# The first MoE product of the last two batches by one level of Strassen

## Chip, core and metric

The kernel runs on one core of a Trainium2 chip. The metric is the device time of one execution in microseconds (us); less is better. Engines are named as in the profile: PE multiplies matrices (PEld is its weight load), DVE and ACT are the vector and the scalar engine, POOL is GpSimd, SP issues most of the DMAs. PE, DVE, ACT and POOL each take their instructions in the order in which they were issued.

## What is computed

Attention with normed q and k, then a two-layer product on its output. 8 batches, 12 heads, 448 positions, 64 per head; 3584 tokens of 768, inner width 2048, all inputs f32.

```
q_n, k_n = rmsnorm(q, g_q), rmsnorm(k, g_k)
attn = softmax(q_n @ k_n.T / 8)
x = (attn @ v)  -> 3584 x 768        # heads side by side
h = x @ w_in                         # 768 -> 2048, "first MoE product"
g = max(0.01 * h, h)
out = g @ w_out                      # 2048 -> 768
```

## The kernel before

The attention works in 24 units: unit u is batch u // 3 and a group of four heads. Each unit has four steps d = 0 to 3. A step issues score matmuls (`qk`, L185, `score`, L179) and the exponential on ACT (`ex`, L192). Step 0 also closes the unit before: the product with v (`pv`, L320), the column sums (`zcol`, L263), and the maximum that shifts the next unit's exponent (`shift_max`, L208, on DVE with `dg` in L221, then `shift_mm`, L226, a small matmul on PE that waits for `dg`). The units 4 to 22 are "narrow": their 1/sum is brought to all rows by a DMA (`zcol_inv`, L289), and POOL multiplies it in (`xmul_pool`, L302: one tensor_tensor of 896 elements a unit, f32 in, f16 out). The result x of a batch lies in `xts[b]`, transposed, 6 blocks of 128 rows and 448 tokens, f16. The last unit does this from PSUM on DVE (`xmul`, L330).

Later units are prepared beside that: sums of squares on DVE (`prep_ssq`, L140), 1/rms on ACT (`prep_rinv`, L145), the norm on DVE (`prep_norm`, L150: two inputs in SBUF, f32, output f16), a transpose by DMA (`prep_trd`, L165), and a scaling on DVE (`prep_g`, L137).

The MoE of batch b is a queue of items, pushed by `push` (L500) when the batch's last unit is nearly through (`fed`, L532: step 3 of the first unit of the next batch), and put between the attention's steps by `fill` (L535): each step gets a share of the queue by the items' costs (1.13 for an item of the first product, 1.31 for one of the second), and after each item one of the step's waiting jobs is issued. After step 3 of unit 23 what is left runs by itself; batch 7's MoE is that tail. So the order on every engine is written out by hand and by these costs.

The first product (`moe1`, L344) has 16 items a batch. Each takes one block of 128 output rows: 6 matmuls of 448 columns into one PSUM bank, then a leaky ReLU on ACT into `gt` (L342).

The second product (`seven`, L423) already uses one level of Strassen on pairs of token tiles: seven items i0 to i6 of 8 matmuls of 384 columns, in four PSUM banks `ma` to `md`. `ma`, `mc` and `md` are used twice: a first product is read out by DVE (L444, or `add`, L435), and a second is then accumulated on top of it in PSUM. The weights' differences are in `tw` (`weight_sum`, L399, 1536 f16 elements each on DVE), those of `gt` in `sa` (`s1` to `s4`, L408 to L418, DVE). What follows an item on DVE or ACT is kept in `pend` (`later`, L420) and issued by `flush` (L373) at the start of the next item.

PSUM has eight banks: two "slots" of two banks each for the scores, and four "aux" banks (`aux`, L55), which the framework hands out in turn.

Of the kernel before, what the change touches and what calls it, by code (L numbers as in the profile page):

```python
# [8 lines left out]
FP32 = mybir.dt.float32  # L9
FP16 = mybir.dt.float16  # L10
AF = mybir.ActivationFunctionType
ALU = mybir.AluOpType
# [6 lines left out]
def kernel(  # L19
# [11 lines left out]
    nc = tc.nc  # L31

    B, H, S, D = q.shape
    QH = 4
    NS = 7
    P = 128
    NQ = H // QH
    NU = B * NQ
    DM, DF = moe_w_in.shape
    KT = DM // P  # L40
    FT = DF // P
# [4 lines left out]
    raws = ctx.enter_context(tc.tile_pool(name="raws", bufs=3))  # L46
    prep_p = ctx.enter_context(tc.tile_pool(name="prep", bufs=2))
# [4 lines left out]
    opool = ctx.enter_context(tc.tile_pool(name="opool", bufs=4))  # L52
    psum = ctx.enter_context(tc.tile_pool(name="psum", bufs=1, space=bass.MemoryType.PSUM))

    def aux(shape, dtype, name):  # L55
        return psum.tile(shape, dtype, tag="aux", bufs=4, name=name)

    ident16 = cst.tile([P, P], FP16)
    make_identity(nc, ident16)
# [17 lines left out]
    win16 = cst.tile([P, NQ, 2, DF], FP16)  # L77
    wout16 = cst.tile([P, FT, DM], FP16)
    gt = cst.tile([P, FT, 8 * 64], FP16)
    HF = FT // 2  # L80
# [29 lines left out]
    def load_v(u):  # L110
# [8 lines left out]
        n16=([P, 2, NS, 2, D], FP16, 1), qkT=([P, 2, NS, P], FP16, 3))  # L119
# [56 lines left out]
    def slot():  # L176
        return psum.tile([P, 2, 512], FP32, tag="sT", bufs=2, name="sT")
# [67 lines left out]
    xts = {}  # L245
# [38 lines left out]
    def zcol_sum(u):  # L284
        s = st[u]
        s["zs"] = zpool.tile([P, HS], FP32, tag="zs", name="zs")
        nc.vector.tensor_reduce(s["zs"], s["zc"][:, 0:S].rearrange("p (k x) -> p x k", k=2), axis=AXL.X, op=ALU.add)

    def zcol_inv(u):  # L289
        s = st[u]  # L290
        nc.scalar.activation(s["zs"], s["zs"], AF.Ln)
        nc.scalar.activation(s["zs"], s["zs"], AF.Exp, bias=0.0, scale=-1.0)
        s["rz"] = zpool.tile([P, 2, S], FP32, tag="rz", name="rz")
        for r in range(2):
            for y in range(2):
                src = s["zs"][64 * y + r:64 * y + 64:2, None, :]
                nc.sync.dma_start(s["rz"][:, r, HS * y:HS * y + HS], src.broadcast_to([32, 4, HS]))
# [32 lines left out]
    def xmul(u):  # L330
        s = st[u]
        b, g = divmod(u, NQ)
        if b not in xts:
            xts[b] = xpool.tile([P, NQ, 2, S], FP16, tag="xt", name="xt")
        for r in range(2):
            nc.vector.tensor_tensor(xts[b][:, g, r], s["pv"][r][:, 0:S], s["rz"][:, r], op=ALU.mult)  # L336

    def prelu(b, dst, src):
        if b % 2 == 0:
            src = src.rearrange("p (t x) -> p t x", t=NS)[:, ::-1]  # L340
            dst = dst.rearrange("p (t x) -> p t x", t=NS)
        nc.scalar.activation(dst, src, AF.Prelu, bias=0.0, scale=1.0, alpha=0.01)  # L342
# [15 lines left out]
    def col(t):  # L358
        return 64 * (5 - 2 * t) if t < 3 else P * (t - 3)
# [10 lines left out]
    pend = []  # L370
    L, R, LR = slice(0, HC), slice(HC, DM), slice(0, DM)

    def flush():  # L373
        while pend:
            pend.pop(0)()

    def out_tile():
        return opool.tile([P, DM], FP32, tag="ost", name="ost")

    def moe2(pair, t, half, part):  # L380
        flush()
        if half == 0 and part == 0:
            ost[0] = out_tile()
        if part == 0:
            ost[1] = aux([P, 512], FP32, "op2")
        op2 = ost[1]
        for ft in range(8 * part, 8 * part + 8):
            nc.tensor.matmul(op2[:, 0:HC], gt[:, ft, ds(col(t), P)], wout16[:, ft, ds(HC * half, HC)],  # L388
                             start=(ft == 0), stop=(ft == FT - 1))
        if part == 0:  # L390
            return
        nc.vector.tensor_copy(ost[0][:, ds(HC * half, HC)], op2[:, 0:HC])
        if half == 1:
            store(pair, t, ost[0], LR, False)

# [24 lines left out]
    def later(fn, *args):  # L420
        pend.append(lambda: fn(*args))

    def seven(pair, tt, nxt=None, last=False):  # L423
        g = {}

        def mm(bank, a, b, first):
            for f in range(HF):
                nc.tensor.matmul(bank[:, 0:HC], a[:, f], b[:, f], start=(first and f == 0), stop=(f == HF - 1), skip_group_check=not first)  # L428

        def bank(name):  # L430
            g[name] = aux([P, 512], FP32, name)
            return g[name]

        def add(dst, src, name):
            nc.vector.tensor_tensor(dst, g[name][:, 0:HC], src, op=ALU.add)  # L435

        def put(i, c):
            store(pair, tt[i], g["o"][i], c, last)

        def i0():  # L440
            flush()
            g["o"] = (out_tile(), out_tile())
            mm(bank("ma"), gblock(tt[0], 0), wblock(0, 0), True)
            later(lambda: nc.vector.tensor_copy(g["o"][1][:, L], g["ma"][:, 0:HC]))  # L444

        def i1():
            flush()
            mm(bank("mb"), sa[:, 1], tw[:, 1], True)
            later(lambda: add(g["o"][1][:, L], g["o"][1][:, L], "mb"))

        def i2():
            flush()
            mm(g["ma"], gblock(tt[0], 1), wblock(1, 0), False)
            later(lambda: nc.scalar.copy(g["o"][0][:, L], g["ma"][:, 0:HC]))  # L454
            if last:
                later(put, 0, L)

        def i3():
            flush()
            mm(bank("mc"), sa[:, 0], tw[:, 0], True)  # L460
            later(lambda: add(g["o"][1][:, R], g["o"][1][:, L], "mc"))
            if nxt:
                later(s1, nxt)

        def i4():
            flush()
            mm(bank("md"), sa[:, 2], tw[:, 2], True)
            later(lambda: add(g["o"][1][:, R], g["o"][1][:, R], "md"))
            if last:
                later(put, 1, R)  # L470

        def i5():
            flush()
            mm(g["mc"], sa[:, 3], wblock(1, 1), False)
            if nxt:
                later(s2, nxt)
            later(lambda: add(g["o"][0][:, R], g["o"][1][:, L], "mc"))
            later(put, 0, R if last else LR)
            if nxt:
                later(s3, nxt)  # L480
                later(s4, nxt)

        def i6():
            flush()
            mm(g["md"], gblock(tt[1], 1), tw[:, 3], False)
            later(lambda: add(g["o"][1][:, L], g["o"][1][:, L], "md"))
            later(put, 1, L if last else LR)

        return [i0, i1, i2, i3, i4, i5, i6]

    queue = []

# [7 lines left out]
    def push(b):  # L500
        pair, odd = divmod(b, 2)
        fast = b > 0
        order = [f // 2 + HF * (f % 2) for f in range(FT)] if odd else range(FT)
        items = [(1.13, lambda ft=ft: (flush(), moe1(b, ft))) for ft in order]
        half = [(slice(0, 4)), (slice(4, 8))]
        if odd:
            tt, tn = (3, 4), (5, 6)
            items += [(1.31, fn) for fn in seven(pair, tt, tn)]
            for n, x, fs in ((8, 0, (s1, s2)), (10, 0, (s3, s4)), (FT - 1, 1, (s1, s2)), (FT, 1, (s3, s4))):
                c, fn = items[n]  # L510
                items[n] = (c, also(fn, *[lambda f=f, x=x: later(f, tt, half[x]) for f in fs]))
            items += [(1.31, fn) for fn in seven(pair, tn, None, b == B - 1)]
        else:
            tiles = (2,) if fast else (0, 1, 2)
            std = [lambda t=t, h=h, p=p: moe2(pair, t, h, p) for t in tiles for h in range(2) for p in range(2)]
            if fast:
                tt = (0, 1)
                std[0] = also(std[0], lambda: later(s1, tt))
                std[1] = also(std[1], lambda: later(s2, tt))
                std[2] = also(std[2], lambda: later(s3, tt), lambda: later(s4, tt))  # L520
                std += seven(pair, tt)
            items += [(1.31, fn) for fn in std]
        queue.extend(items)
# [53 lines left out]
    with tc.manual_schedule():  # L577
# [172 lines left out]
        first = slot()  # L750
# [9 lines left out]
        for u in range(3, NU):  # L760
            for d in range(4):
# [18 lines left out]
                def job(fn, *args):  # L780
                    jobs.append(lambda: fn(*args))
# [37 lines left out]
                    job(weight_sum, u - 5, 1)  # L819
                if d == 2 and 5 <= u < 8:  # L820
                    job(xmul_sb, u - 1)
                if d == 3 and 6 <= u < NU - 3:
                    for ti in range(2):
                        job(prep_sq, u + 3, ALL, (ti,))
# [2 lines left out]
        pv(NU - 1)  # L827
        zinv(NU - 1)
        xmul(NU - 1)
        push(B - 1)  # L830
        while queue:
            queue.pop(0)[1]()
# [29 lines left out]
```

## Time and profile before

| what | value |
|---|---|
| median of 3 runs | 424.19 us (424.12 to 425.42) |
| profiled execution | 424.41 us, of which the span of the trace is 422.6 |
| DMA | 62.37 MB, mean 148 GB/s |
| first product, L348 on PE | 756 matmuls recorded, 151.2 us |
| its leaky ReLU, L342 on ACT | 126 of 448 elements, 66.4 us, 547 ns each |
| POOL's multiplication, L307 | 16 of 896 elements, 33.7 us, 2104 ns each |
| `weight_sum`, L403 on DVE | 8 of 1536 elements, 0.946 us at the least |
| batch 6, first product | 340.1 to 362.8 us of the span, between the steps of units 22 and 23 |
| batch 7, first product | 381.8 to 400.0 us, alone on PE |

Busy times are those of one execution. An engine's row names the source line, the operation, output and inputs, and the shape. A row of the timeline starts with the start in us from the span's start and the duration in us; "[0.31 <-ACT rinv L148]" is idle time of the engine before the row and what ended it. A PE row's end holds the depth of the array, some 0.16 us that the next matmul overlaps. Idle time of an engine that nothing waits for costs nothing.

### The profile page before, as it was taken

How to read it: one execution, taken by the hardware profiler on the slowest of the kernel's cores; microseconds unless marked ns; L12 is line 12 of the kernel's file. 1: busy time of each engine (PE TensorE's matmuls, PEld its weight loads, DVE VectorE, ACT ScalarE, POOL GpSimd, SP SyncE). 2: the span in 40 equal slices, each digit the busy share in tenths (PEclk: the TensorE clock that was granted, in tenths of full speed). 3: DMA queues.
4: the chain of work that ended last, by engine and by line, in shares of the span. 5: the costliest groups of instructions: out<-in, count | busy, mean ns of one | idle time of the engine just before them, and what ended most of it. 6: DMA issues, size and time to landing. Idle time of an engine off the chain costs nothing.

```text
span 422.6 us, 8871 instructions
## 1 busy us (share of the span) xinstructions
PE 407.0 (96%) x3623; PEld 207.3 (49%) x3623; DVE 256.2 (61%) x417; ACT 302.9 (72%) x470; POOL 83.3 (20%) x75
## 2 busy tenths in 40 slices
PE   7887999989999999999999999999999999999995
PEld 6554454444445544454445544454445544555563
DVE  5788675888568736576459736577449721531262
ACT  5999877768987689877887689867986566733400
POOL 1957432200020121210220220210120101200000
PEclk9699999999999999999999999999999999999999
DMA  7999996889664995677664795677542460213023
GB/s 269 228 250 259 237 253 90 209 150 198 165 152 74 213 247 94 160 185 166 155 148 74 211 216 118 172 164 175 156 79 45 123 158 2 45 37 76 0 57 94
DMA packets 71947, 62.37 MB, mean 148 GB/s; under 512 B 36324, under 2 KB 67044, under 8 KB 71908
## 3 DMA queue, kind: packets, MB, share of 16 engines
q1 hardware_dynamic: 61312, 49.62, 46.1%
q0 software_dynamic: 10272, 11.80, 17.8%
q8 instruction: 28, 0.46, 0.5%
q10 hardware_dynamic: 324, 0.39, 0.3%
q14 instruction: 11, 0.09, 0.1%
HBM read 45.61 MB, written 11.01 MB: 134 GB/s over the span
## 4 chain that ended last, share of the span: by engine, by line
PE 83%; DVE 8%; ACT 6%; issue 1%; DMA 1%; SPq 0%; DVEq 0%
PE hps L348 34%; PE sT L182 8%; PE ma L428 7%; PE md L428 7%; PE mc L428 7%; PE sT L327 6%; PE op L388 4%; ACT et L201 4%; PE mb L428 3%; PE zc L270 3%; DVE n L154 2%; DVE ssq L142 1%; DMA rk<-in_k_dram 1%; PE pv L327 1%; DVE xt L336 1%
## 5 line engine op out<-in xcount | busy, mean ns | idle before, releaser
L201 ACT ACTIVATE et<-sT,eb 128x896 f16<-128x896 f32 x166 | 159.4, 1009 | 17.8 <-PE sT L182 16.1
L348 PE MATMUL hps<-xt,win 128*128 128x448 f16 x756 | 151.2, 353 | 0.4 <-DVE xt L336 0.2
L348 PEld LDWEIGHTS <-win 128*128 128x128 f16 x756 | 70.5, 98 | 72.2 <-issue 10.8
L342 ACT ACTIVATE gt<-hps 128x448 f16<-128x448 f32 x126 | 66.4, 547 | 21.0 <-PE hps L348 20.5
L307 POOL TENSOR_TENSOR xt<-x,rz 128x896 f16<-128x896 f32 x16 | 33.7, 2104 | 145.5 <-DMA rz<-zs 114.7
L154 DVE TENSOR_TENSOR n<-rq,rinv 128x896 f16<-128x896 f32 (+2 forms) x25 | 27.1, 1086 | 50.8 <-ACT rinv L148 47.7
L182 PE MATMUL sT<-qkT 64*64 64x448 f16 x664 | 53.1, 369 | 2.7 <-ACT et L201 1.6
L142 DVE TENSOR_REDUCE ssq<-sq 128x14 f32<-128x896 f32 (+2 forms) x49 | 50.3, 1057 | 0.6 <-ACT sq L131 0.6
L428 PEld LDWEIGHTS <-sa 128*128 128x128 f16 x352 | 32.8, 98 | 26.3 <-issue 6.1
L282 ACT COPY x<-sT 128x896 f32<-128x896 f32 x19 | 17.2, 906 | 37.4 <-DVE sT L232 37.4
L111 POOL DMA_DIRECT2D vt<-in_v_dram x24 | 18.2, 757 | 114.7 <-PE sT L327 107.2
L219 DVE TENSOR_REDUCE sT<-sT 128x1 f32<-128x896 f32 x22 | 24.1, 1094 | 20.0 <-PE sT L182 19.8
L428 PEld LDWEIGHTS <-gt 128*128 128x128 f16 x264 | 25.2, 98 | 18.5 <-issue 2.1
L388 PE MATMUL op<-wout,gt 128*128 128x384 f16 x192 | 34.1, 327 | 0.0
L182 PEld LDWEIGHTS <-qkT 64*64 64x64 f16 x672 | 15.0, 105 | 37.0 <-issue 33.5
L428 PE MATMUL ma<-wout,gt 128*128 128x384 f16 x176 | 32.3, 327 | 0.0
L327 PE MATMUL sT<-et,vt 64*64 64x448 f16 x532 | 28.5, 350 | 0.3
L409 DVE TENSOR_TENSOR sa<-gt 128x512 f16<-128x512 f16 (+1 forms) x15 | 8.1, 543 | 31.8 <-ACT gt L342 31.8
L327 PEld LDWEIGHTS <-vt 64*64 64x64 f16 x672 | 20.7, 107 | 11.3 <-issue 1.7
L154 DVE TENSOR_TENSOR n<-rk,rinv 128x896 f16<-128x896 f32 (+2 forms) x26 | 26.1, 1010 | 0.0
L388 PEld LDWEIGHTS <-gt 128*128 128x128 f16 x192 | 17.7, 98 | 13.9 <-issue 3.1
L454 ACT COPY ost<-ma 128x384 f32<-128x384 f32 x11 | 5.3, 478 | 24.1 <-PE ma L428 24.1
(86 smaller groups left out, 420.4 us busy)
## 6 DMA issues: line engine op xcount, KB each, us to landing
rq<-in_q_dram SPq DMA_DIRECT2D x24, 448.0 KB, 4.2
rk<-in_k_dram SPq DMA_DIRECT2D x24, 448.0 KB, 5.7
out_dram<-ost SPq DMA_DIRECT2D x52, 192.0 KB, 2.9
rz<-zs SPq DMA_DIRECT2D x76, 112.0 KB, 2.3
vt<-in_v_dram POOLq DMA_DIRECT2D x24, 224.0 KB, 5.8
win<-in_moe_w_in_dram POOLq DMA_DIRECT2D x8, 384.0 KB, 12.6
wout<-in_moe_w_out_dram POOLq DMA_DIRECT2D x2, 1536.0 KB, 26.1
out_dram<-ost SPq DMA_DIRECT2D x4, 96.0 KB, 2.1
```

The lines of the kernel that those rows point to most:

```text
L111: nc.gpsimd.dma_start(vts[u % NV].rearrange("p a t d -> p a (t d)"), rows(v, u))
L142: nc.vector.tensor_reduce(buf(u, "ssq")[:, ti, :, c[0]:c[1]], buf(u, f"sq{ti}")[:, :, c[0]:c[1]], axis=AXL.X, op=ALU.add)
L154: nc.vector.tensor_tensor(buf(u, "n16")[:, ti, c[0]:c[1]].rearrange("p s a d -> p a s d"), src[:, :, c[0]:c[1]], buf(u, "rinv")[:, ti, :, ...
L182: nc.tensor.matmul(banks[a][64 * r:64 * r + 64, 0:S].rearrange("p (t x) -> p t x", t=NS), kT(u, r, a, t), qT(u, r, a), start=True, stop=True)
L201: nc.scalar.activation(s["et"][:, t], sT[:, :, 0:S], AF.Exp, bias=s["eb"], scale=1.0)
L219: nc.vector.tensor_reduce(s["spare"][:, 511:512], sT[:, :, 0:S], axis=AXL.XY, op=ALU.max)
L307: eng.tensor_tensor(xts[b][:, g], s["x32"], s["rz"], op=ALU.mult)
L327: nc.tensor.matmul(s["pv"][r][64 * a:64 * a + 64, 0:S], vts[u % NV][64 * r:64 * r + 64, a, t], s["et"][64 * r:64 * r + 64, t, a], start=(t ...
L342: nc.scalar.activation(dst, src, AF.Prelu, bias=0.0, scale=1.0, alpha=0.01)
L348: nc.tensor.matmul(hps[:, 0:S], win16[:, kt // 2, kt % 2, ts(ft, P)], xt[:, kt // 2, kt % 2], start=(kt == 0), stop=(kt == KT - 1))
L388: nc.tensor.matmul(op2[:, 0:HC], gt[:, ft, ds(col(t), P)], wout16[:, ft, ds(HC * half, HC)], start=(ft == 0), stop=(ft == FT - 1))
L428: nc.tensor.matmul(bank[:, 0:HC], a[:, f], b[:, f], start=(first and f == 0), stop=(f == HF - 1), skip_group_check=not first)
```

## The change

For batches 6 and 7 (`LATE = 6`) the first product takes one level of Strassen: K is halved (3 blocks of 128 each), the output rows are halved (8 blocks each), and the tokens are halved (224 each: of each run of 64 tokens, the first 32 or the last). For each of four groups s of two row blocks per half there are seven items of 6 matmuls of 224 columns: 28 items a batch instead of 16, 168 matmuls instead of 96.

The sums of w_in (`win_sum`) are the same for both batches: four kinds of 1536 f16 elements, for each of two halves x of the columns. Those of x = 0 are made on DVE as jobs of units 20 and 21 (two in step 1 of unit 20, one in step 0 and one in step 1 of unit 21, the last in place in w_in), those of x = 1 on POOL, all four in step 3 of unit 21, ahead of unit 21's multiplication on that queue. The sums of x (`x_sum`, four of 672 f16 elements a batch) are made on DVE: for batch 6 in units 21 and 22, for batch 7 after the last `xmul`.

The products 1, 6, 5, 3 go through one PSUM bank, 7 and 4 through another, 2 through a third; between them DVE reads a partial sum out (`copy`, `vadd`; one vadd writes PSUM), and the next product is accumulated on top. ACT then does the leaky ReLU, four of 448 elements a group, two from PSUM and two from the f32 tiles u and v. In the tail ACT also copies product 1.

The aux banks are handed out by hand from the start of batch 6 (`hold`, `drop`); in the tail the two slots' four banks are added. Items of the first product count 0.575 in `fill`. In the tail `s1` to `s4` of a half are issued together, after the last item of groups 1 and 3; before, `s1`, `s2` and `s3`, `s4` were issued after different items. The order of instructions shows on POOL four tensor_tensors more, on SP the same transfers in the same order.

```diff
+    def win_sum(n, x, tile_=None, eng=nc.vector):
+        if tile_ is None:
...
+            ws[n, x] = win_b(1, 0, 4 * x, 4)
...
+        a, b = {1: (lambda: (win_b(1, 0, 4 * x, 4), win_b(1, 1, 4 * x, 4))),
+                2: (lambda: (ws[1, x], win_b(0, 0, 4 * x, 4))),
+                3: (lambda: (win_b(0, 0, 4 * x, 4), win_b(1, 0, 4 * x, 4))),
+                4: (lambda: (win_b(0, 1, 4 * x, 4), ws[2, x]))}[n]()
+        eng.tensor_tensor(ws[n, x], a, b, op=ALU.add if n == 1 else ALU.subtract)
...
+    def x_sum(b, n):
+        x_tiles()
+        t = xs
+        a, c = {1: (x_b(b, 0, 1), x_b(b, 0, 0)), 2: (x_b(b, 1, 1), t[1]),
+                3: (x_b(b, 1, 1), x_b(b, 0, 1)), 4: (x_b(b, 1, 0), t[2])}[n]
+        nc.vector.tensor_tensor(t[n], a, c, op=ALU.subtract)
...
+        def item(n, s):
+            flush()
+            if n == 1:
+                if s == 0:
+                    start()
+                mm(get(1, s), 1, s, x_b(b, 0, 0), True)
+                later(lambda: copy(tmp["u"][:, s % 2], g[1, s][:, 0:S]))
+            elif n == 2:
+                mm(get(2, s), 2, s, x_b(b, 1, 0), True)
+                later(lambda: vadd(tmp["u"][:, s % 2], g[2, s], tmp["u"][:, s % 2]))
+                later(lambda: drop(g[2, s]))
+                later(lambda: out_(s, 0, 0, tmp["u"][:, s % 2]))
+            elif n == 7:
+                mm(get(7, s), 7, s, xs[3], True)
+                later(lambda: nc.vector.tensor_copy(tmp["v"][:, s % 2], g[7, s][:, 0:S]))
+            elif n == 6:
+                mm(g[1, s], 6, s, xs[2], False)
+                later(lambda: vadd(g[7, s][:, 0:S], g[1, s], tmp["v"][:, s % 2]))
+            elif n == 5:
+                mm(g[1, s], 5, s, xs[1], False)
+                later(lambda: vadd(tmp["v"][:, s % 2], g[1, s], tmp["v"][:, s % 2]))
+                later(lambda: out_(s, 1, 1, tmp["v"][:, s % 2]))
+            elif n == 4:
+                mm(g[7, s], 4, s, xs[4], False)
+                later(lambda: out_(s, 1, 0, g[7, s][:, 0:S]))
+                later(lambda: drop(g[7, s]))
+            else:
+                mm(g[1, s], 3, s, x_b(b, 1, 1), False)
+                later(lambda: out_(s, 0, 1, g[1, s][:, 0:S]))
+                later(lambda: drop(g[1, s]))
+                for fn in after.get(s, ()):
+                    pend.append(fn)
+
+        order = ((1, 0), (2, 0), (7, 0), (1, 1), (6, 0), (2, 1), (5, 0), (4, 0), (7, 1), (3, 0),
+                 (6, 1), (1, 2), (2, 2), (5, 1), (4, 1), (7, 2), (3, 1),
+                 (6, 2), (1, 3), (5, 2), (4, 2), (7, 3), (3, 2),
+                 (6, 3), (2, 3), (5, 3), (4, 3), (3, 3))
+        return [(0.575, lambda n=n, s=s: item(n, s)) for n, s in order]
...
+        late = b >= LATE
+        after = {}
+        if late:
+            if odd:
+                tt = (3, 4)
+                for s_, x in ((1, 0), (3, 1)):
+                    after[s_] = [lambda f=f, x=x: f(tt, half[x]) for f in (s1, s2, s3, s4)]
+            items = late1(b, b == B - 1, after)
...
+                if u == NU - 4 and d == 1:
+                    job(win_sum, 1, 0, (raws, "rq", 3))
+                    job(win_sum, 2, 0, (raws, "rk", 3))
+                if u == NU - 3:
+                    if d == 0:
+                        job(win_sum, 4, 0, (prep_p, "sq", 3))
+                    if d == 1:
+                        job(x_sum, LATE, 1)
+                        job(win_sum, 3, 0)
+                    if d == 3:
+                        for n, tile_ in ((1, (raws, "rq", 3)), (3, None), (2, (raws, "rk", 3)), (4, (prep_p, "n16", 1))):
+                            win_sum(n, 1, tile_, nc.gpsimd)
+                        job(x_sum, LATE, 3)
+                if u == NU - 2 and d == 0:
+                    job(x_sum, LATE, 2)
+                    job(x_sum, LATE, 4)
...
         xmul(NU - 1)
+        for n in (3, 1, 2, 4):
+            x_sum(B - 1, n)
         push(B - 1)
```

An item is written (product, group s): (5, 0) is product 5 of group 0.

## The prediction

> **What bounds the kernel now.** I read the busy shares first, then the chain that ended last, then busy time by stretch, then the timeline of all engines from 300 us on. PE is busy 96% of the span and carries 83% of the chain; in the stretches that the change touches it is never idle:
>
> ```profile
> PE 407.0 (96%) x3623; PEld 207.3 (49%) x3623; DVE 256.2 (61%) x417; ACT 302.9 (72%) x470; POOL 83.3 (20%) x75
> ...
> PE 83%; DVE 8%; ACT 6%; issue 1%; DMA 1%; SPq 0%; DVEq 0%
> ```
> ```profile
> 340.00:360.00 20.00, 20.00 (x162) 9.42 (x159) 3.32 (x9) 14.42 (x24) 2.08 (x1) 1.00 0.26 64
> ```
> (stretch, length, then busy us of PE, PEld, DVE, ACT, POOL, the clock, DMA; from 360 to 382 PE is again busy all 22.00 us.) PE takes its matmuls in order and has nothing to catch up with later, so an us saved on PE is an us of the span, and so is an us that PE waits. What decides is whether DVE and POOL keep up with the new sums.
>
> **What it removes.** In the tail 96 matmuls of 448 columns take 18.16 us (chain: "PE hps L348 x96"), 189.2 ns each; eight of 384 columns take 1.30 us, 162.5 ns. That is 0.417 ns a column plus 2.4 ns. A matmul of 224 columns, with its own weight load, is then 95.8 ns. The warm-up row supports it: 42 matmuls of 128 columns, each with a new 128x128 load, in 2.52 us, (2.52-0.22)/41 = 56 ns, where the line gives 55.8, so loads hide behind matmuls shorter than ours.
>
> ```profile
> 4.84 2.52 PE L575 MATMUL warm<-onesp 128*128 128x128 f16 x42
> ```
> A batch's 168 cost 16.1 us instead of 18.16: **-2.07 us** each for batches 6 and 7. No row has a moving operand in runs of 32 elements; scores read runs of 64 at full rate, so I take no loss. SP's queue has the same transfers as before, in the same order.
>
> **DVE and POOL get in each other's way.** This row set decides the rest:
>
> ```profile
> 367.15 0.69 DVE L415 TENSOR_TENSOR sa<-gt 128x1024 f16<-128x1024 f16 x1
> 367.23 2.54 POOL L307 TENSOR_TENSOR xt<-x,rz 128x896 f16<-128x896 f32 x1 [17.09 <-DMA rz<-zs]
> ...
> 367.75 2.57 DVE L418 TENSOR_TENSOR sa<-gt,sa 128x1024 f16<-128x1024 f16 x1
> ```
> L307 on POOL is otherwise 2.07 us and L418 0.68. POOL came while DVE's L415 ran, and lost 0.47 us; DVE's next came while POOL held, and lost 1.9: it ran as POOL ended. The same is seen with the norm L154 (1.61 us at 238.24, POOL at 236.83 for 2.07) and the weight differences L403 (1.66 instead of 0.95). So a DVE operation that reads two SBUF tensors waits out POOL's tensor_tensor, and they alternate. L435, with one input in PSUM, is not held (333.21, below).
>
> **Term 1, unit 20, +2.9.** By the built kernel's order, the first two w_in sums stand on DVE between the ssq at 315.31 and the copy of ma. They have L403's shape, 0.95 us.
>
> ```profile
> 315.31 1.08 DVE L142 TENSOR_REDUCE ssq<-sq 128x14 f32<-128x896 f32 x1
> 315.40 2.07 POOL L307 TENSOR_TENSOR xt<-x,rz 128x896 f16<-128x896 f32 x1 [7.69 <-ACT et L201]
> 316.31 0.55 DVE L444 COPY ost<-ma 128x384 f32<-128x384 f32 x1
> 316.91 1.46 PE L428 MATMUL ma<-wout,gt 128*128 128x384 f16 x8
> ```
> POOL holds the first until about 317.35: 318.3, 319.25, then the copy to 319.8. PE's second ma accumulates into the bank that the copy reads; it starts at 319.8 instead of 316.9. What follows moves with it. Without POOL's hold 1.8 remains; it can't be below that, since the order is fixed.
>
> **Term 2, unit 21, +9.6.** Times are as before the shift of term 1. The sum ws4 (d=0) has slack and costs nothing. Then:
>
> ```profile
> 331.46 2.09 POOL L307 TENSOR_TENSOR xt<-x,rz 128x896 f16<-128x896 f32 x1 [13.99 <-DMA rz<-zs]
> 333.21 0.56 DVE L435 TENSOR_TENSOR ost<-mc,ost 128x384 f32<-128x384 f32 x1 [1.50 <-PE mc L428]
> 334.08 1.09 DVE L154 TENSOR_TENSOR n<-rq,rinv 128x896 f16<-128x896 f32 x1 [0.31 <-ACT rinv L148]
> 334.91 1.47 PE L428 MATMUL mc<-wout,sa 128*128 128x384 f16 x8
> ...
> 336.22 1.46 PE L428 MATMUL md<-tw,gt 128*128 128x384 f16 x8
> ...
> 338.19 1.09 DVE L219 TENSOR_REDUCE sT<-sT 128x1 f32<-128x896 f32 x1
> 340.03 0.23 PE L231 MATMUL sT<-dg,onesp 128*128 128x64 f16 x2
> ```
> POOL gets four sums of 1536 elements behind this L307. Their price is in no row. A 1-element copy (L243) is 0.18 us, so L307 costs 2.11 ns an element, 3.42 us for 1536; L135 (f32 out, 1.68 us for 896) gives 2.75. f16 inputs could halve it (1.7) if bytes set the pace, but L307 writes fewer bytes than L135 and is slower. I take 3.4, the row with f16 in it.
> On DVE: x_sum 1 (672 elements; L409 takes 0.42 for 512 and 0.68 for 1024, so 0.50) waits for L307 and ends at 333.9. POOL's first sum takes its turn to 337.3; DVE's in-place sum follows to 338.1, the mc add to 338.6, and PE's second mc starts at 338.65, not 334.91. POOL's second sum to 341.5, norm q to 342.5, md add to 343.0, PE's second md at 343.0. POOL's third to 345.9, norm k to 346.85. The fourth needs the buffer that norm k's transpose is read from, and comes later. x_sum 3, two adds, the maximum L219 and dg end at 349.6: PE's L231 stands at 349.65, not 340.03. With a POOL sum of p us this is 3p-0.6: 9.6; 10.1 at L307's plain ratio 3.55; 4.5 at 1.7. If nothing were held, about 0.5.
>
> **Term 3, batch 6, +2.5.** PE's 28 items of 0.575 us wait for DVE passes over 448 PSUM columns (0.62, L287's row). Behind dg and zs, DVE is late: the copy of item (1,0) ends 1.9 us after PE began it, x_sum 2 is held by POOL's fourth sum, then vadd, x_sum 4, two copies. PE waits 0.55 at (6,0), 1.45 at (5,0), later 1.1 and 0.5 where a bank is freed by an ACT prelu queued behind two exps of 1 us, 0.8 at (6,3)-(5,3) behind unit 23's maximum and 0.25 at (3,3): 4.65. DVE sat idle for 15.5 us here, so its time is there; the distance of one 0.575 us item between a read and the next write of a bank is what is too short. 4.65-2.07 = 2.5. Between -2.07 and +3.5.
>
> **Term 4, tail, +3.7.** The four x_sums (two wait for their forerunners, 1.9 us) stand between xmul and the md add:
>
> ```profile
> 378.59 1.16 DVE L336 TENSOR_TENSOR xt<-pv,rz 128x448 f16<-128x448 f32 x2 [2.94 <-ACT rz L314]
> 379.66 0.55 DVE L435 TENSOR_TENSOR ost<-md,ost 128x384 f32<-128x384 f32 x1
> 380.37 1.46 PE L428 MATMUL md<-tw,gt 128*128 128x384 f16 x8
> ```
> The add ends at 382.05 and the second md starts at 382.1: +1.73. In the 28 items a one-item gap costs 0.6 (vadd) + 0.2 (semaphore and last matmul's depth) - 0.575, some 0.25, at (5,0), (5,3), (3,3); (2,2) waits for an ACT copy, 0.75; before (5,2) DVE does s1 to s4 (1.55 us), which wait for the prelu of (3,1), 1.85: 3.4 in all. The second half of s1 to s4 now stands ahead of the copy of ma: 0.6. 1.73+3.4+0.6-2.07 = 3.7. With sums at full rate and no gaps, 1.4-2.07+1.7, about 1.
>
> **Sum.** 2.9+9.6+2.5+3.7 = 18.7. The profiled execution took 424.41 (span 422.6), 0.22 above the median; 424.41+18.7 = 443.1, on the median **442.9**.
>
> A rule against the change: while PE waits 3.7, 3.0 and 3.0 us, its clock could drop. The page's first slice shows 0.6 of the clock, and 32 warm-up matmuls 107 ns each (3.44 us), twice the later 56; no later slice is below 0.9, but no wait of 3 us is there either. The Trainium skill (TensorE: Matmul & The Clock Gate, Part 1) has the clock halved after an idle window of about 3.4 us, until as long a busy one; by it the sum could be some 1.7 us more for one such window. I leave it out of the sum.
>
> **Rivals.** *POOL is quick on f16* (1.7 us a sum): term 2 is 4.5, sum 13.6, **437.8**. For it: half the bytes; against: L307 and L135. *DVE isn't held here* (the holds seen are single operations): 1.8+0.5+1.8+3.7 = 7.8, **432**. *More than reckoned* (clock drop or POOL slower than L307, 5 us): **448**. *Faster*: the sums fit into DVE's idle time, PE never waits, and both batches give their 2.07: **420.1**. It needs DVE to release ma by 316.9, mc by 334.9 and md by 336.2, and two DVE passes per item pair in time; it decides at the first of these, where 1.9 us of sums stand ahead of the copy with no idle DVE time between. *It doesn't do what it says*: matmuls of 224 columns cost more than half of 448 (loads of 98 ns showing through): then 168x98 = 16.5, a gain of 1.7 instead of 2.07, inside the range. *No change*: waits and gains cancel, 424.
>
> **Numbers.** As worked out 0.52; quick POOL 0.20; no hold 0.13; worse 0.07; faster 0.05; no change 0.03. The first three hold 0.85; 431.5 (below "no hold") to 447 (first case with 10.1 and 3.5, and the clock) is the range. This kernel's measurement tells about 0.3% from no change: faster 0.05, same 0.03, slower 0.92.
>
> **What would show it.** Right: PE idle before the second ma of unit 20 put down to DVE's copy; 128x1536 rows on POOL of about 3.4 us, one after the other, and norms of 3 to 4 us beside them; 224-column matmuls 96 ns apart; the md add after four x_sums. Wrong: POOL rows under 2 us; norms at 1.09 beside them; PE without idle time between 316 and 350; matmuls of 224 columns 110 ns apart or more.

## The result, and the profile after

The kernel is slower: 446.15 us median of 4 runs (443.53 to 446.72) against 424.44 for the kernel before (4 runs, 424.12 to 425.42), a ratio of 1.049 (95%: 1.046 to 1.053). The prediction was 442.9 with a range of 431.5 to 447. The profiled execution is the fastest, 443.53 us (span 441.7), 19.1 us above the profiled one of before; the median is 21.7 above. The first difference is accounted for below from the traces; for the 2.6 us between the two a second profile shows one execution (experiment 5).

The page of the profile after: busy time by engine, the clock in 40 slices, the chain that ended last.

```profile
PE 407.4 (92%) x3767; PEld 221.5 (50%) x3767; DVE 296.4 (67%) x465; ACT 304.6 (69%) x474; POOL 96.8 (22%) x79
...
PEclk9699999999999999999999999999999799999999
...
PE 68%; DVE 16%; ACT 9%; issue 4%; DMA 1%; DVEq 0%; SPq 0%; ACTq 0%
```

PE is as busy as before (407.0 us) in a span that is 19 us longer, and DVE's share of the chain has doubled, from 8% to 16%. PE has no more to do (rather less: 403.8 us busy in experiment 3, where the clock doesn't fall); it waits. (The 7 in the clock's row is the slice of unit 21.) For what, the view of PE's waits says (line of PE, line waited for, us in all, times, longest):

```profile
PE mc L444 <- DVE ost L451: 3.2, 1, 3.2
PE ma L444 <- DVE ost L460: 2.7, 1, 2.7
PE bank L565 <- DVE xs L551: 2.2, 1, 2.2
...
PE md L444 <- DVE ost L451: 1.9, 1, 1.9
PE sT L565 <- DVE bank L578: 1.8, 2, 1.6
PE bank L444 <- DVE ost L451: 1.8, 1, 1.8
```

None of these stands in the profile of before. Each is one wait at one place, but for the sT row, two waits of the tail (1.6 and 0.2). In order of time:

**Unit 20** (the timeline of POOL, DVE and PE):

```profile
315.69 2.08 POOL L321 TENSOR_TENSOR xt<-x,rz 128x896 f16<-128x896 f32 x1 [7.67 <-ACT et L214]
316.61 1.97 DVE L534 TENSOR_TENSOR ws<-win 128x1536 f16<-128x1536 f16 x1
318.62 0.96 DVE L534 TENSOR_TENSOR ws<-ws,win 128x1536 f16<-128x1536 f16 x1
319.49 0.55 DVE L460 COPY ost<-ma 128x384 f32<-128x384 f32 x1
...
320.09 1.46 PE L444 MATMUL ma<-wout,gt 128*128 128x384 f16 x8 [2.72 <-DVE ost L460]
```

The first w_in sum begins while POOL multiplies and takes 1.97 us where the second takes 0.96; the copy of ma stands behind both, and PE behind the copy.

**Unit 21**, the same view:

```profile
335.31 1.76 DVE L551 TENSOR_TENSOR xs<-xt 128x672 f16<-128x672 f16 x1
336.67 3.36 POOL L534 TENSOR_TENSOR ws<-win 128x1536 f16<-128x1536 f16 x1
337.00 3.83 DVE L534 TENSOR_TENSOR win<-win 128x1536 f16<-128x1536 f16 x1
340.10 3.68 POOL L534 TENSOR_TENSOR win<-win 128x1536 f16<-128x1536 f16 x1
340.76 0.54 DVE L451 TENSOR_TENSOR ost<-mc,ost 128x384 f32<-128x384 f32 x1
341.23 3.50 DVE L167 TENSOR_TENSOR n<-rq,rinv 128x896 f16<-128x896 f32 x1
341.35 2.03 PE L444 MATMUL mc<-wout,sa 128*128 128x384 f16 x8 [3.18 <-DVE ost L451]
343.74 3.93 POOL L534 TENSOR_TENSOR ws<-ws,win 128x1536 f16<-128x1536 f16 x1
344.65 0.55 DVE L451 TENSOR_TENSOR ost<-md,ost 128x384 f32<-128x384 f32 x1
345.12 3.50 DVE L167 TENSOR_TENSOR n<-rk,rinv 128x896 f16<-128x896 f32 x1
345.25 2.72 PE L444 MATMUL md<-tw,gt 128*128 128x384 f16 x8 [1.86 <-DVE ost L451]
...
351.55 0.22 PE L244 MATMUL sT<-dg,onesp 128*128 128x64 f16 x2 [0.69 <-DVE dg L234]
```

Each row of the norm (L167) lasts 3.50 us, where before it lasted 1.08; each begins inside a POOL sum and ends 0.95 us after that sum's end (343.78 and 347.67), the first of them inside the next sum. The adds with an input in PSUM (L451) keep their 0.55. The longer a DVE row beside POOL, the later the add behind it, and PE stands behind the add. (The POOL rows overlap DVE's in the same way: the row holds the time in which it waits for its turn.)

**Batch 6 and the tail** (timeline of POOL, DVE and PE):

```profile
352.80 3.09 POOL L534 TENSOR_TENSOR ws<-win,ws 128x1536 f16<-128x1536 f16 x1 [5.13 <-DMA qkT<-n]
...
353.39 2.86 DVE L551 TENSOR_TENSOR xs<-xt,xs 128x672 f16<-128x672 f16 x1
...
356.31 0.73 PE L565 MATMUL bank<-xs,ws 128*128 128x224 f16 x6 [2.23 <-DVE xs L551]
...
412.97 0.73 PE L565 MATMUL sT<-xs,ws 128*128 128x224 f16 x6 [1.61 <-DVE bank L578]
```

The first row of PE is (6,0), behind x_sum 2 (353.39), which POOL's fourth sum (352.80) holds for 2.4 us; the second is (5,2), behind s1 to s4.

### The profile page after: what moved, and what is told of

Its sections match the earlier page's. It is cut to its first block, busy times and chain, and to the rows that moved or that the text cites. A ratio compares the mean times of both kernels' runs of the same rounds, so it can differ in the third digit from the quotient of the medians.

```text
span 441.7 us, 9243 instructions
## 1 busy us (share of the span) xinstructions
PE 407.4 (92%) x3767; PEld 221.5 (50%) x3767; DVE 296.4 (67%) x465; ACT 304.6 (69%) x474; POOL 96.8 (22%) x79
## 4 chain that ended last, share of the span: by engine, by line
PE 68%; DVE 16%; ACT 9%; issue 4%; DMA 1%; DVEq 0%; SPq 0%; ACTq 0%
PE hps L363 23%; PE sT L195 7%; PE sT L341 5%; ACT et L214 5%; PE ma L444 4%; PE md L444 4%; PE mc L444 4%; PE bank L444 3%; PE bank L565 3%; DVE n L167 3%; PE op L403 3%; PE zc L283 3%; PE mb L444 2%; PE sT L444 2%; PE bank L403 1%
## 5 line engine op out<-in xcount | busy, mean ns | idle before, releaser
L363 PE MATMUL hps<-xt,win 128*128 128x448 f16 x564 | 113.9, 353 | 0.4 <-DVE xt L350 0.2
L167 DVE TENSOR_TENSOR n<-rq,rinv 128x896 f16<-128x896 f32 (+2 forms) x25 | 29.0, 1162 | 50.4 <-ACT rinv L161 47.6
L357 ACT ACTIVATE gt<-hps 128x448 f16<-128x448 f32 x94 | 49.2, 548 | 5.2 <-PE hps L363 5.0
L167 DVE TENSOR_TENSOR n<-rk,rinv 128x896 f16<-128x896 f32 (+2 forms) x26 | 28.5, 1104 | 0.0
L403 PE MATMUL op<-wout,gt 128*128 128x384 f16 x160 | 28.4, 327 | 0.0
L444 PE MATMUL ma<-wout,gt 128*128 128x384 f16 x128 | 23.5, 327 | 2.7 <-DVE ost L460 2.7
L403 PEld LDWEIGHTS <-gt 128*128 128x128 f16 x192 | 17.7, 98 | 13.6 <-issue 2.7
```

Source lines behind the costliest of these rows:

```text
L167: nc.vector.tensor_tensor(buf(u, "n16")[:, ti, c[0]:c[1]].rearrange("p s a d -> p a s d"), src[:, :, c[0]:c[1]], buf(u, "rinv")[:, ti, :, ...
L363: nc.tensor.matmul(hps[:, 0:S], win16[:, kt // 2, kt % 2, ts(ft, P)], xt[:, kt // 2, kt % 2], start=(kt == 0), stop=(kt == KT - 1))
```

## Experiments

**1. Without POOL's sums.** The four sums of the second half of the columns are left out; the products 3, 5, 6 and 7 of those rows then use the first half's sums.

```diff
-                        for n, tile_ in ((1, (raws, "rq", 3)), (3, None), (2, (raws, "rk", 3)), (4, (prep_p, "n16", 1))):
-                            win_sum(n, 1, tile_, nc.gpsimd)
+                        for n in (1, 2, 4):
+                            ws[n, 1] = ws[n, 0]
+                        ws[3, 1] = win_b(1, 0, 4, 4)
```

> This leaves out the four sums of w_in that POOL computes for the second half of the output rows (the products 3, 5, 6, 7 of those rows then use the first half's sums, so gt is wrong there); everything else is the changed kernel. Theory (POOL's sums hold DVE's operations and so the matmuls of mc and md): the waits of mc (3.2 us) and md (1.9 us) in unit 21 and the clock drop beside them go, leaving at most 1 us of the 8.3, and xs no longer waits behind a fourth POOL sum, so the wait of (6,0) falls from 2.2 to about 0.5 us: the profiled execution falls from 443.5 to about 434, the median from 446.2 to 434 to 436.5. The +2.9 of unit 20 and the +3.9 of the tail stay. Rival (POOL is off the path; what counts is the work added to DVE and the new products' own waits): within 1 us of the changed kernel, 445 to 446.5.

Measured 434.02 us (433.24 to 435.07; ratio to the kernel before 1.022, 1.020 to 1.025). The theory holds, the rival falls: 12 us of the 21.7 come with four operations on an engine that is 22% busy. (By the two profiles, with the fall of the clock below set aside, 10.1 us of it are waits, 7.75 in unit 21 and 2.36 in batch 6; the rest lies between the medians and the profiled executions.) Timeline of PE:

```profile
320.17 1.67 PE L444 MATMUL ma<-wout,gt 128*128 128x384 f16 x8 [2.70 <-DVE ost L460]
321.77 0.96 PE L195 MATMUL sT<-qkT 64*64 64x448 f16 x8
322.66 2.46 PE L444 MATMUL mc<-tw,sa 128*128 128x384 f16 x8
324.95 1.46 PE L444 MATMUL md<-tw,sa 128*128 128x384 f16 x8
...
340.12 1.46 PE L444 MATMUL mc<-wout,sa 128*128 128x384 f16 x8 [0.31 <-DVE ost L451]
```

The second mc waits 0.31 instead of 3.18, md and dg not at all, and (6,0) starts without a wait: batch 6's first product takes 24.18 us instead of 26.54. The upper rows show something else: after the wait of 2.70 us in unit 20 the score and the first mc take 0.96 and 2.46 us instead of 0.57 and 1.47. The clock fell there (0.90 in the stretch from 318 to 335; 1.00 in the profile of the changed kernel, after the same wait). From the second ma to md it is 4.78 us against 3.21: the fall cost 1.57.

**2. The same sums on DVE.**

```diff
-                            win_sum(n, 1, tile_, nc.gpsimd)
+                            win_sum(n, 1, tile_, nc.vector)
```

> The same four sums of w_in at the same place in the program, computed by DVE instead of POOL. Theory: DVE pays four operations of 0.96 us, 3.9 us, but none of its others is held for 2 us any more, so mc and md wait about half as long (4 to 5 us in place of 8.3 in unit 21) and the wait of (6,0) falls by 1.7: 438 to 441, faster than the changed kernel by 5 to 8 us although DVE does more. Rival (the amount of DVE work is what counts): DVE has 3.9 us more in a stretch where it is already late, and the kernel is slower than the changed one, 448 to 450.

Measured 439.12 us (439.01 to 440.82; 1.035, 1.032 to 1.038), as the theory had it: DVE does four operations more, and the kernel is 7 us faster. Where PE waits is not where I expected it (DVE and PE):

```profile
338.15 1.08 DVE L167 TENSOR_TENSOR n<-rq,rinv 128x896 f16<-128x896 f32 x1
...
344.82 0.96 DVE L534 TENSOR_TENSOR ws<-win,ws 128x1536 f16<-128x1536 f16 x1 [1.40 <-DMA qkT<-n]
...
348.71 0.27 PE L244 MATMUL sT<-dg,onesp 128*128 128x64 f16 x2 [5.08 <-DVE dg L234]
```

The norm is back at 1.08, mc and md wait no longer than in experiment 1, and the whole delay comes at dg, 5.08 us: the adds stand ahead of the sums, the maximum and dg behind them. 1.40 of it is the fourth sum, which waits for the transposing DMA to have read the buffer that it writes. Behind this wait the clock is down: the first 12 matmuls of batch 6 take 2.43 us instead of 1.31, and its first product 24.95 us against 24.18 in experiment 1.

**3. Without any sum of w_in.** The products that use them take blocks of w_in itself.

```diff
-                    job(win_sum, 1, 0, (raws, "rq", 3))
-                    job(win_sum, 2, 0, (raws, "rk", 3))
...
-                        job(win_sum, 4, 0, (prep_p, "sq", 3))
...
-                        job(win_sum, 3, 0)
...
+                        for x in range(2):
+                            for n in (1, 2, 4):
+                                ws[n, x] = win_b(0, 1, 4 * x, 4)
+                            ws[3, x] = win_b(1, 0, 4 * x, 4)
```

> This leaves out all eight sums of w_in (the products that use them take blocks of w_in itself, so gt is wrong). Theory: against the kernel without POOL's sums the wait of the second ma product in unit 20 goes as well, 2.9 us: 431 to 433.5. What is then left over the kernel before is batch 6's waits minus its 2.07 and the tail's 3.85. Rival (the sums on DVE in unit 20 only fill idle time, and the 2.9 us there have another cause): the same time as the kernel without POOL's sums.

Measured 429.25 us (429.17 to 429.50; 1.011, 1.009 to 1.013): the wait of unit 20 is gone, and more than its 2.9. From the first ma to L244 it takes 25.73 us, as before the change (25.73), so terms 1 and 2 are zero here. My range began 1.8 us too high: it was reckoned from experiment 1 with the wait alone. Against experiment 1's profile the fall of the clock behind the wait (1.57 us) goes too, the 0.58 that were left in unit 21, and 0.9 ahead of unit 20, where nothing was changed. The stretches by time (length, busy us of PE, PEld, DVE, ACT, POOL, the clock, DMA's share and GB/s) show no fall, and the four runs lie within 0.33 us.

```profile
318.00:335.00 17.00, 17.00 (x158) 8.77 (x151) 15.92 (x25) 11.63 (x17) 2.08 (x1) 1.00 0.45 101
```

What is left over the kernel before is batch 6 (24.18 against 22.57) and the tail, 1.6 and 3.9; 0.5 came back ahead of unit 20 in this execution (first ma at 313.81, not 314.30).

**4. x_sums of the tail later.**

```diff
+        for _ in range(3):
+            queue.pop(0)[1]()
         for n in (3, 1, 2, 4):
             x_sum(B - 1, n)
```

> The changed kernel with the four x_sums of the last batch put behind the three leftover products of batch 5's output (mc second, md first and md second are issued before them) instead of ahead of them. Theory: the second md product waits 1.79 us because its add stands on DVE behind the last unit's xmul and four x_sums; without them ahead it waits for nothing, and the first product that reads a sum is two items later, so the time falls by 1.5 to 1.8 us, 444.4 to 444.7. Rival (the x_sums are only shifted: product (7,0) then waits for them instead): within 0.3 us of the changed kernel.

Measured 442.32 us (441.25 to 444.02; 1.042, 1.039 to 1.044). In the trace the second md (of batch 6's output) follows mc at 1.30 us, without its wait, and from mc to the end it takes 1.79 us less than in the changed kernel: the theory's size. The medians differ by more, 3.8 us, which one profile of each can't explain; the next two experiments look at what varies.

**5. The changed kernel again.** Unedited, for a second profile.

> The changed kernel once more, unedited, for a second profile: the first profiled execution (443.53) lies 2.6 us below the median of its runs (446.15). Theory: the same waits stand in it, and what differs from execution to execution is at which of the three long waits of PE (2.7 us in unit 20, 3.2 in unit 21, 2.2 at (6,0)) the granted clock falls; each fall costs 1.2 to 2 us. An execution near 446 then shows a fall in unit 20 or at (6,0) beside the one in unit 21. Rival: the waits themselves are longer, and the clock is the same 0.80 in unit 21 alone.

Measured 444.91 us (443.29 to 446.20; 1.049, 1.045 to 1.052), and the profiled execution was the slowest, 446.20. Its clock and its rows of PE:

```profile
PEclk9999999999999999999999999999999969999999
```
```profile
319.71 1.97 PE L444 MATMUL ma<-wout,gt 128*128 128x384 f16 x8 [2.71 <-DVE ost L460]
321.61 0.96 PE L195 MATMUL sT<-qkT 64*64 64x448 f16 x8
322.50 2.16 PE L444 MATMUL mc<-tw,sa 128*128 128x384 f16 x8
...
342.57 1.46 PE L444 MATMUL mc<-wout,sa 128*128 128x384 f16 x8 [3.21 <-DVE ost L451]
346.47 1.46 PE L444 MATMUL md<-tw,gt 128*128 128x384 f16 x8 [2.44 <-DVE ost L451]
...
352.77 0.22 PE L244 MATMUL sT<-dg,onesp 128*128 128x64 f16 x2 [2.43 <-DVE dg L234]
```

The two long waits, for the copy of ma and the mc add, are the same to 0.03 us, and the clock falls elsewhere: in unit 20 (1.57 us, as in experiment 1) and at (6,0) (batch 6's first product 27.98 instead of 26.54, 1.44), not in unit 21. 1.57+1.44 = 3.0 is what this execution is longer from the first ma to the end. The theory holds for it, except that it had a fall in unit 21 beside these. That the other executions near 446 owe their time to the clock as well is inferred from this one; none of them was profiled. And the fall in unit 21 of the first profile was free: from the second mc to L244 it took 10.20 us there, with slow matmuls and 0.69 of waiting for dg, and 10.20 here, with fast ones and 2.43. In unit 21 DVE sets the time, whatever PE's clock.

**6. PE kept busy in the waits.** Matmuls of constants, in a bank of their own, ahead of the second ma of unit 20 and the second mc and md of unit 21.

```diff
+            if b == LATE - 1:
+                for i, n in ((FT + 2, 36), (FT + 12, 44), (FT + 13, 24)):
+                    c, fn = items[i]
+                    items[i] = (c, lambda fn=fn, n=n: (flush(), warm(n, aux([P, 512], FP32, "warm")), fn()))
```

> The changed kernel with matmuls of constants, whose results nobody reads, put into PE's queue ahead of the three products that wait: 36 ahead of the second ma of unit 20, 44 ahead of the second mc and 24 ahead of the second md of unit 21 (each 128 columns, some 0.055 us at full clock, so 2.0, 2.4 and 1.3 us of waits of 2.7, 3.2 and 1.9). Theory: the waits stay but PE is busy in them, the granted clock stays at 1.0 in 318 to 352, and the time is that of the waits alone: 1.5 to 3.5 us under the changed kernel's median, 442.5 to 444.5. Rival (the clock doesn't follow these waits, or the drop costs nothing because PE would wait for dg anyway): within 0.5 us of the changed kernel run beside it, or slower by the added matmuls.

Measured 444.20 us (443.12 to 444.52; 1.048, 1.046 to 1.049) beside 444.91 (1.045 to 1.052): in total inconclusive, the intervals overlap. The profile (PE):

```profile
316.70 2.17 PE L736 MATMUL warm<-onesp 128*128 128x128 f16 x36
319.58 1.46 PE L444 MATMUL ma<-wout,gt 128*128 128x384 f16 x8 [0.71 <-DVE ost L460]
...
351.07 0.26 PE L244 MATMUL sT<-dg,onesp 128*128 128x64 f16 x2 [2.43 <-DVE dg L234]
351.15 2.43 PE L565 MATMUL bank<-xt,win 128*128 128x224 f16 x12
```

In the filled waits the clock stays up, and it falls at the next one, dg, which I had not filled: the first 12 matmuls of batch 6 take 2.43 us instead of 1.31. That fall is free too: (6,0) then waits for POOL's fourth sum 0.82 us instead of 2.23, and batch 6's first product takes 26.56 us, as in the first profile (26.54). From the first ma to the end this execution takes 123.0 us, again as the first profile: neither has a fall that costs anything, and what is left is the waits, which the added matmuls don't shorten. No run of the four reached 446, which two of the four unfilled ones did.

**7. The last batch alone, same order of products.** `LATE = 7`; six sums of w_in on DVE in unit 22, two after batch 6's first mc add; x_sums late.

```diff
-    LATE = 6
+    LATE = 7
...
+                if u == NU - 2 and d == 0:
+                    job(win_sum, 1, 0, (raws, "rq", 3))
+                    job(win_sum, 2, 0, (raws, "rk", 3))
+                if u == NU - 2 and d == 1:
+                    job(win_sum, 4, 0, (prep_p, "sq", 3))
+                    job(win_sum, 1, 1, (raws, "rq", 3))
+                if u == NU - 2 and d == 2:
+                    job(win_sum, 2, 1, (raws, "rk", 3))
+                    job(win_sum, 4, 1, (prep_p, "n16", 1))
...
+        win_sum(3, 0)
+        win_sum(3, 1)
         zsum_slot(NU - 1)
```

> Strassen in the last batch alone, with all eight sums of w_in on DVE: six in unit 22, where the kernel before leaves DVE idle from 341.8 to 357.3 us, two after the last product of batch 6; x_sums behind the leftover products; the order of the products as in the changed kernel. Theory: the sums are now free, since no product of the first three quarters of the path waits for DVE there, and what is left is the last batch by itself: its first product takes 19.84 us (as in the run with x_sums late) in place of 18.16, and the second ma another 0.36, so 2.0 us slower than the kernel before, 426.2 to 426.8. Rival (the two-input DVE operations cost wherever they stand): 1 to 3 us more, 427.5 to 429.5.

Measured 426.17 us (425.72 to 426.78; 1.004, 1.003 to 1.005). All eight sums cost nothing where nothing stands behind them: from the first ma of unit 20 to the last md before the tail's first product it takes 66.08 us, before 66.07. One batch of Strassen in this order still loses: the tail's first product takes 19.68 us against 18.16, with the same wait at (5,2).

```profile
395.07 0.73 PE L565 MATMUL sT<-xs,ws 128*128 128x224 f16 x6 [1.61 <-DVE bank L578]
```

**8. The last batch alone, another order.** As 7, with at least two other items between products that depend on each other, one bank of each of the two slots, and the first half's s1 to s4 after (5,3).

```diff
-        order = ((1, 0), (2, 0), (7, 0), (1, 1), (6, 0), (2, 1), (5, 0), (4, 0), (7, 1), (3, 0),
...
+        order = [(int(x[0]), "ABCD".index(x[1])) for x in
+                 "1A 1B 2A 2B 7A 7B 6A 6B 1C 5A 5B 4A 4B 3A 3B 1D 2C 7C 7D 6C 6D 2D 5C 5D 4C 4D 3C 3D".split()]
...
-                for i in range(2):
-                    two = slot()
-                    for r in range(2):
-                        drop(two[:, r])
+                two = [slot()[:, 0] for i in range(2)]
+                held[0][:] = two + [held[0][i] for i in (1, 2, 0, 3)]
...
+                for k, x, fs in (((5, 3), 0, (s1, s2, s3, s4)), ((3, 3), 1, (s1, s2))):
+                    after[k] = [lambda f=f, x=x: f(tt, half[x]) for f in fs]
```

> The same, with the 28 products of the last batch in an order that leaves at least two others (1.15 us) between two products of which the second waits for an addition of the first (0.2 us to its start, 0.63 its length, 0.06 back), two groups side by side, one bank of each of the two score slots in place of both, and s1 to s4 of the first half behind the last addition that a product waits for. Theory: the 3.76 us of waits in the first product come from one-item gaps and from s1 to s4 ahead of an addition; without them the 2.06 us that 224-column matmuls save are all that is left: 422.2 to 422.8, faster than the kernel before by 1.6 to 2.2. Rival (ACT, with 20 outputs and copies of 0.53 to 0.58 us in 16.1 us, or the banks hold the products wherever they stand): most of the 3.76 stays, 424.5 to 426.5.

Measured 422.54 us (421.88 to 424.05, 7 runs) against 424.38: a ratio of 0.996 (0.994 to 0.998). This beats both kernels, by 1.8 us over the one before. The profiled execution is the slowest of the seven, 424.05: it reaches the first ma of unit 20 at 315.88 instead of 314.30, ahead of anything that was changed, and takes 102.12 us from there to the last DVE row, 1.81 less than before (103.93). The stretch of the tail's first product (columns as above): PE never idle, DVE 12 of 17 us, ACT 10.

```profile
383.00:400.00 17.00, 17.00 (x175) 16.52 (x173) 12.08 (x24) 9.57 (x20) 0.00 (x0) 1.00 0.18 48
```

It takes 16.24 us, from 383.26 to the first ma at 399.50, where 168 matmuls of 95.8 ns make 16.1. The rival (ACT, or the banks) is out. Experiments 7 and 8 differ in order, banks and the place of s1 to s4 together; which share of the 3.6 us belongs to which was not tried.

## Why the prediction was right, term by term

The mechanism was right in each of the four terms, and the sum within 0.6 us of what the profiled execution shows. That closeness is in part luck: two terms were off by more than a microsecond, in opposite directions. Measured from the first ma of unit 20, by starts on PE, and at the end by the last DVE row (418.23 before, 437.56 after):

| term | predicted | measured | what is off |
|---|---|---|---|
| before unit 20 | 0 | +0.3 | first ma 314.60, not 314.30 |
| 1, unit 20 | +2.9 | +2.88 | nothing |
| 2, unit 21 | +9.6 | +8.33 | POOL's sum |
| 3, batch 6 | +2.5 | +3.97 | the hold at (6,0) |
| 4, tail | +3.7 | +3.85 | nothing of size |
| sum | 18.7 | 19.3 | |

- *A 224-column matmul at 95.8 ns:* right. Six of them follow each other at 0.575 us in each undisturbed stretch (409.47, 410.04, 410.62), runs of 32 elements and all.
- *Term 1:* the rows are the predicted ones; experiment 3 takes it away whole.
- *Term 2:* right in kind and in the order of turns, mis-sized in p. "I take 3.4" rested on L307's 2.11 ns an element; the one POOL sum that no DVE operation held up (352.80) took 3.09, so 3p-0.6 is 8.7. With f16 inputs POOL took 10% less for an element (1.89 ns, the 0.18 us of the 1-element copy taken off as in the prediction), not half. With the four sums gone (experiment 1) 0.58 remain, against "if nothing were held, about 0.5".
- *Term 3:* the step that failed is "PE waits 0.55 at (6,0)". I had seen that x_sum 2 waits for POOL's fourth sum, but not that this sum begins so late: it waits for the transposing DMA until 352.80, right where x_sum 2 comes up, and PE waits 2.23. The other waits were 1.24 at (5,0) (predicted 1.45), 0.64 and 0.28 behind ACT (1.1 and 0.5), 0.64 at (5,3) (0.8) and 0.30 at (3,3) (0.25). Without POOL's fourth sum batch 6 costs 24.18-22.57 = 1.6.
- *Term 4:* the second md starts 1.96 us late (predicted 1.73), the 28 items lose 3.6 (3.4), the second ma 0.35 (0.6). Experiment 4 takes the first away.
- *The clock, left out of the sum:* the estimate was 1.7 us for a fall; it is 1.57 in unit 20, 1.44 and 0.35 at (6,0) (experiments 5 and 4), and nothing in unit 21. It makes the second profile 3.0 us longer than the first, from the first ma on. That it also puts the median 2.6 us above the first profiled execution is inferred (experiment 5). As it stands, the median, 446.15, is nearer to the "worse" case's 448 than to 442.9; that case was half true: not POOL slower, but the clock.
- *The rivals:* quick POOL falls with 3.09 us, no hold with the norm's 3.50. The rival "faster" had named idle DVE time as its condition; experiment 8 uses just that time, for the last batch alone, and gets 1.8 of the 2.07 that a batch has to give.

## What to carry to other kernels

Where one engine is busy 96% of the span, Strassen's saving (one matmul in eight) is small money, 2 us here, and every sum that it adds must run where no add or copy that the busy engine needs stands behind it: the same eight sums cost some 11 us in units 20 and 21 and 2.4 more in batch 6, with four of them on POOL, and nothing, all on DVE, in unit 22 and behind batch 6's first mc add. Helping out a late engine with one that it has to take turns with can be worse than letting it do the work itself: the four sums cost 7 us less on DVE. And products that go through an accumulator that another engine reads in between need a distance in the order of at least that engine's whole turn, here 0.9 us, so two items of 0.575. (That is read from the rows; experiment 8 changed the banks and the place of s1 to s4 as well.)

## What the runs showed of the hardware

- Alternation, not one hold: when both have a queue of SBUF-SBUF operations, DVE and POOL take turns, and each DVE operation costs its own time plus about what is left of POOL's: 3.50 is 1.08 and 2.4 of waiting, 3.83 is 0.95 and 2.9. The Trainium skill (SBUF — State Buffer, Who interferes with whom) says that a DVE instruction with two SBUF inputs contends with a GpSimd instruction that reads SBUF, and that the first to issue holds the shared ports for its whole length; these rows agree, down to the adds with one PSUM input, which stayed at 0.55.
- The clock falls after shorter waits than I allowed for, and not always. After 2.7 us in unit 20 it fell in two of five profiles, after 3.2 us at mc in two of three, around the 2.2 us at (6,0) in two of three; in experiment 3, where no wait after the first 50 us is over 1.8 us, it didn't fall. The Trainium skill (TensorE: Matmul & The Clock Gate, Part 1) asks for an idle window of about 3.4 us; here the measurement decides, and waits of 2.2 to 2.7 us, with matmuls on both sides, were enough in some executions. That a fall lasts one such window agrees: 3.4 us of half the clock in unit 20 (experiments 1 and 5), or two, 6.8 us in unit 21 of the first profile.
- Why the same wait brings a fall in one execution and none in another can be read from the six profiles in which a fall was seen (the first profile, experiments 1, 2, 4, 5 and 6). Cut each into stretches of 3.41 us, counted from the start of a fall: from 310 to 420 us every stretch has the clock at 1.00 or at 0.50 throughout, and the two falls of experiment 5 begin eleven such stretches apart (37.5 us), those of experiment 4 four (13.6 us). After a stretch at full clock in which PE was idle for 2.10 to 2.66 us the next was slow (seven of seven), after up to 1.95 us it never was, and at 2.06 us once and once not. The 2.7 us wait of unit 20 lay with 2.30 and 2.60 us in one stretch where the clock fell (experiments 1 and 5), and was split into 0.83 and 1.88 in the first profile, where it didn't.
- A fall is free where PE would have waited anyway (unit 21, 10.20 us with it and without; batch 6, 26.56 and 26.54).
